# Linear attention with a rational feed-forward layer: the low words of 28 slots on GpSimd, Square and Ln in two buffers, another order

## The chip, the cores and the metric

The kernel runs on one core of one Trainium2 chip. The metric is the device time of one execution in microseconds (us). A core has five engines that run beside each other, each in its own program order: TensorE (PE in the profile), VectorE (DVE), ScalarE (ACT), GpSimd (POOL) and SyncE (SP), which here issues most DMAs.

## The reference, cut to what matters

A linear attention with decay over 4 x 8 heads of 768 steps gives x, 3072 tokens by 384. A feed-forward layer with a rational function of h follows.

```python
for t in range(S):
    cur = einsum('bhd,bhe->bhde', u * k[t], v[t])
    y[t] = einsum('bhd,bhde->bhe', r[t], state + cur)
    state = w * state + einsum('bhd,bhe->bhde', k[t], v[t])
...
h = x @ w_in                       # 3072 x 2048
P = a[0] + a[1]*h + a[2]*h*h + a[3]*h*h*h
Q = 1 + |b[0]|*|h| + |b[1]|*h*h
out = (P / (Q + 1e-6)) @ w_out     # 3072 x 384
```

## The kernel before

**Attention.** The 768 steps of each of 4 batches are cut into 6 blocks of 128, which makes 24 blocks n. For each block SP loads r, k and v (tasks Lr, Lk, Lv, and LV for a copy of v in another layout). r and k are scaled by powers of the decay (sr, sk), the bonus term is formed (ba, bb, bs, bv), PE transposes (tk, tr) and multiplies (a, kv, y), and ACT or DVE move results out of PSUM (tke, tre, ae, kve, ye). ca carries the state on. x turns the result, and xh and xl split it into a high and a low word, since each product of the feed-forward layer is made of three passes: high by high, high by low and low by high.

**Feed-forward.** Two blocks make a tile of 256 tokens, 12 tiles in all. The 2048 columns of h are worked on in 50 slots s (the table SL), most of them 1024 wide: four groups of 128 columns by 256 tokens. f1 (L644) makes h in PSUM, 9 matmuls of 256 columns for each group. Only two buffers of PSUM hold h (h0 and h1, in turn), so f1 of slot s+2 waits until the buffer of slot s is free. Then come ten instructions on the whole slot:

| task | line | engine | does | writes |
|---|---|---|---|---|
| z | L670 | ACT | absolute value of h | q |
| q | L674 | ACT | Square, so that q is Q without its last constant | q |
| t | L679 | ACT | Square of h, shifted | z |
| u3 | L691 | DVE | (t + constant) * h: P without its last constant | h, in PSUM |
| ln | L683 | ACT | Ln of q | z |
| ex | L687 | ACT | Exp(-z), which is 1/Q | z |
| hi | L696 | DVE | (h + constant) * z: the high word of P/Q | g |
| p | L700 | DVE | (q + constant) * g | q |
| d | L704 | DVE | h + constant - q: what the high word leaves over | h, in PSUM |
| lo | L709 | DVE | h * z: the low word | l |

t and ln share a buffer: ln overwrites what t wrote, so it waits until u3 has read it. q, z, g and l lie in seven SBUF buffers of 1024 columns (tags ta0 to ta6). f2 (L648, L649, L650) multiplies the two words by w_out, in two halves of 128 tokens, 12 matmuls of 384 columns each; the lines are high by high, high by low and low by high. os moves a finished half out of PSUM (L756 on ACT, L760 on DVE) and od stores it (L764).

**Weights.** w_in and w_out come as 64-bit numbers, in 28 pieces. Each is loaded by cl, turned into float32 by c0, cu (ACT), c2, c3 (DVE) and cr (POOL), and split by ch (ACT) and co (L420).

**Order.** Nothing is scheduled at build time. A string, ORDER, lists some 1840 tasks, each with the letter of its engine (D, A, G, P, S) and its buffer, and each engine takes its tasks in that order. The task warm.n (L797) is n matmuls on a constant, whose result nobody reads; they stand where PE has nothing else to do.

Of the kernel before, what the change touches and what calls it, by code (L numbers as in the profile page):

```python
# [49 lines left out]
pad.1G coefS plG mskG st0.0G st0.1G idG pad.0G wS Lv.3S betaA uwS ubG warm.54P ubpPpa0 cl_D ctrA st0.2A st0.3A Lv.2S LV.1.1.0A  # L50
LV.1.0.0A Lr.1S sqD Lr.2S pad.2G pow.0D pow.1D warm.10P turn.0.0Ppa1 warm.6P turn.1.0P inv.0D Lr.0S ubeA warm.13P turn.0.1Ppa0
pow.2D LV.1.0.1A Lk.0S Lk.2S warm.4P turn.2.0P tab.0A sr.1G inv.1D inv.2D warm.29P turn.2.1P Lk.1S Lv.0S LV.1.1.1A wlD turn.1.1P
tab.1A cl.2S tr.1Ph0 tre.1.0A tre.1.1A sr.0D wpPpa1 w128A cl.5S sr.2D sk.0D sk.2D ba.2Dm0 tr.0Ppa0 tre.0.1A warm.9P kv.2Ph1 sk.1D
tre.0.0A kve.2.0A bb.2D ba.0Dm1 Lr.3S ba.1Gm2 bs.2D bv.2D Lv.1S tk.0Ph0 tke.0A c0.2A c2.2Dh0 bb.1G kv.0Ppa1 kve.0.1A warm.2P
a.0Ppa0 bb.0G kve.2.1A warm.6P tk.1Ph1 c3.2D cu.2A cr.2Gta0 Lk.3S cl.6S tke.1A warm.16P a.1Ph0 kve.0.0A tk.2Ppa1 ae.0.1D cl.12S
bs.0D c0.5A ch.2A ae.0.0D bv.0G bs.1D LV.0.1.1A cl.1S ae.1.0D Lr.4S c2.5Dh1 LV.0.0.1A LV.0.0.0A ae.1.1D warm.36P kv.1Ph0 cl.4S
sr.3G c3.5D LV.0.1.0A y.0Ppa0 sk.3G ba.3Dm3 co.2D c0.6A bb.3D Lk.5S ca.0.1G cu.6A Lk.4S kve.1.0A c2.6Dh1 tke.2A ye.0D ca.0.0G
kve.1.1A c3.6D cr.6Gta1 c0.12A c2.12Dh0 c3.12D bv.1D warm.7P tr.2Ppa1 warm.2P kv.3Ppa0 c0.1A c2.1Dh1 c3.1D tre.2.0A cu.12A
cr.12Gta2 tre.2.1A bs.3D warm.13P x.0Ph0 cl.26S kve.3.0A kve.3.1A cu.5A warm.11P a.2Ppa1 ae.2.0D sr.4G y.1Ph1 tr.3Ppa0 ch.12A
cl.0S cu.1A sk.5G ae.2.1D ca.1.1G c0.4A warm.5P y.2Ppa1 ye.1D tk.3Ph1 xh.0A sk.4D tre.3.1A ca.1.0D xl.0D warm.3P tr.4Ph0 c0.26A  # L60
Lr.5S tre.3.0A tke.3A cr.5Gta3 ye.2D ba.4Dm1 c0.0A ch.6A warm.2P x.2Ppa0 xh.2A bv.3G c2.26Dh1 c3.26D cu.4A cr.1Gta4 xl.2D a.3Ppa1
warm.2P tk.4Ph1 ae.3.1D tre.4.0A sr.5G cl.20S Lv.5S tre.4.1A warm.21P kv.5Ph0 bb.4G cl.3S cl.9S ch.5A co.5G ae.3.0D c2.0Dpa0 c3.0D
ch.1A co.1G Lv.4S cu.20A tke.4A bs.4D c0.20A cl.10S cu.3A cl.11S kve.5.1D cu.0A cr.0Gta5 c2.4Dpa1 c3.4D cr.4Gta6 warm.16P x.1Ph1
xh.1A c0.3A xl.1D a.4Ppa0 warm.20P kv.4Ph1 cu.9A c2.3Dpa1 c3.3D cl.15S ch.0A co.0G cr.3Gta0 cu.26A cr.26Gta3 cl.14S cl.8S kve.5.0D
kve.4.1D c0.10A c2.10Dh0 c3.10D kve.4.0D warm.3P tk.5Ppa1 tke.5A cu.10A warm.14P y.3Ppa1 ye.3D c0.11A cu.11A ch.3A ba.5Gm0 c0.15A
f1.0.0Ph0 bv.4G LV.2.0.0S c2.11Dpa1 c3.11D cr.11Gta4 cu.15A LV.2.1.1S x.3Ph1 xh.3A ch.26A c0.9A c2.15Dpa1 c0.14A f1.0.1P f1.0.2P
bb.5G co.26G LV.2.1.0S ch.11A xl.3D tr.5Ph1 tre.5.1A tre.5.0A c3.15D co.12G ae.4.1D LV.2.0.1S ae.4.0D Lr.6S c2.14Dpa1 bs.5D
f1.0.3P warm.6P f1.1.0Ph1 cl.24S Lr.7S c3.14D z.0Ata5 c2.20Dpa0 c3.20D t.0Ata3 u3.0D warm.7P a.5Ppa1 ch.4A cu.8A cl.27S warm.1P
y.4Ppa0 cl.7S cl.13S ae.5.0D q.0A ln.0A f1.1.1P co.6G bv.5G cr.15Gta2 ch.15A ye.4D warm.5P x.4Ppa0 xh.4A cr.20Gta1 ch.20A Lk.6S
ae.5.1D warm.6P y.5Ppa1 sr.6D ex.0A cl.21S xl.4D warm.1P tr.6Ppa0 tre.6.0A tre.6.1A co.15G co.20G f1.1.2P f1.1.3P cl.18S ye.5D  # L70
c0.7A hi.0Dta2 x.5Ppa0 cl.17S sr.7G p.0D d.0D co.4G c0.8A z.1Ata1 xh.5A xl.5D tr.7Ppa1 tre.7.0A tre.7.1A co.3G lo.0Dta5 warm.54P
f1.2.0Ph0 f1.2.1P t.1Ata6 c2.9Dpa0 cr.10Gta0 ch.10A sk.6G cl.25S u3.1D co.10G co.11G Lr.8S c2.8Dpa1 f1.2.2P f1.2.3P ca.2.1G c3.9D
q.1A ln.1A ex.1A c0.17A c3.8D cr.8Gta3 cu.13A c2.7Dpa0 cl.16S cu.14A f2.0.0P f2.0.1P cl.22S cl.23S Lk.7S c0.13A hi.1Dta0 tk.6Ppa1
Lk.8S cu.7A ch.8A os.0.0A c3.7D z.2Ata4 t.2Ata2 ca.2.0G p.1D d.1D lo.1Dta5 co.8G cr.7Gta1 c2.17Dpa0 c3.17D sr.8G c2.13Dh1 os.0.1A
warm.23P f2.1.0P f2.1.1P q.2A cr.9Gta6 ch.7A co.7G Lv.8S u3.2D c0.16A c2.16Dpa0 c3.16D c3.13D ch.9A co.9G ca.3.0G warm.6P
f1.3.0Ph1 c0.18A c2.18Dpa0 c3.18D ln.2A ex.2A c0.23A cu.17A cr.14Gta3 cu.23A tke.6A c0.21A os.1.0A ch.14A Lv.6S warm.1P kv.6Ppa0
hi.2Dta0 p.2D d.2D lo.2Dta5 cu.16A cr.13Gta1 ch.13A co.13G co.14G c2.21Dpa1 kve.6.1D sk.7G f1.3.1P f1.3.2P f1.3.3P t.3Ata6 z.3Ata4
q.3A warm.16P f1.4.0Ph0 f1.4.1P c3.21D a.6Ppa1 u3.3D ln.3A ex.3A kve.6.0D ba.6Gm2 Lk.9S os.1.1A ba.7Gm3 Lr.10S c2.23Dpa0 ae.6.0D
cr.16Gta2 ch.16A c3.23D hi.3Dta1 p.3D f1.4.2P f1.4.3P t.4Ata3 c0.25A warm.1P tk.7Ppa0 f2.2.0P os.2.0A co.16G d.3D sk.8G bb.7G
Lv.7S c0.27A bb.6G lo.3Dta2 LV.3.0.1S f2.2.1P z.4Ata4 u3.4D q.4A ln.4A ex.4A ae.6.1D warm.8P f1.5.0Ph1 f1.5.1P f1.5.2P f1.5.3P  # L80
bs.6D os.2.1A f2.3.0P cr.23Gta6 ch.23A co.23G bs.7D c2.27Dpa1 c3.27D hi.4Dta0 c0.22A c2.22Dpa1 t.5Ata5 p.4D d.4D f2.3.1P cu.25A
# [855 lines left out]
```

## Time and profile before

| | |
|---|---|
| runs | 567.09 us (median of 3; 566.33 to 570.7) |
| the profiled execution | 566.86 us, its span 565.1 us |
| mean granted TensorE clock | 0.997 |
| busy | PE 550.0, DVE 471.7, ACT 397.0, POOL 163.1 us |
| loaded and stored | 29.01 MB and 4.72 MB |

The span runs from the first to the last instruction; 1.8 us of the execution lie outside it. Busy time of PE counts a matmul from its start to a modelled end, and since matmuls overlap, a short wait between two of them does not show in it. A wait is put down to the engine and line that released it.

### The profile page before, as it was taken

The page shows a single profiled execution, that of the slowest core. Times are in us where ns is not written, and L with a number is a line of the kernel's source. Part 1 is how long each engine was busy: PE and PEld are TensorE (multiplying, and loading weights), DVE is VectorE, ACT ScalarE, POOL GpSimd, SP SyncE. Part 2 cuts the span into 40 slices and gives each one's busy share as a digit, 9 for nine tenths or more (in the row PEclk, how much of TensorE's full clock was granted, in tenths as well). Part 3 has the DMA queues.
Part 4 walks back from the last instruction along what each step waited for, and adds up shares of the span by engine and source line. Part 5 has one row for each costly group of instructions (what it writes and reads, how often), then busy time and mean ns, then how long its engine had stood idle before and what let it go on. Part 6 is the DMA issues. An engine that isn't in the chain of part 4 may idle for free.

```text
span 565.1 us, 13792 instructions
## 1 busy us (share of the span) xinstructions
PE 550.0 (97%) x5916; PEld 527.3 (93%) x5916; DVE 471.7 (83%) x576; ACT 397.0 (70%) x522; POOL 163.1 (29%) x189
## 2 busy tenths in 40 slices
...
POOL 5689776688323143132121010001100100100000
PEclk9999999999999999999999999999999999999998
...
DMA packets 95273, 34.69 MB, mean 61 GB/s; under 512 B 88546, under 2 KB 91620, under 8 KB 95204
## 3 DMA queue, kind: packets, MB, share of 16 engines
...
q14 instruction: 21, 0.17, 0.1%
HBM read 29.01 MB, written 4.72 MB: 60 GB/s over the span
## 4 chain that ended last, share of the span: by engine, by line
PE 71%; DVE 17%; ACT 6%; issue 3%; POOL 1%; DVEq 0%; ACTq 0%; POOLq 0%
PE h L644 26%; PE o L648 8%; PE o L650 8%; PE o L649 8%; PE y L600 4%; DVE q L700 4%; PE a L550 4%; DVE g L696 4%; PE kv L572 4%; DVE h L704 3%; PE idle_bank L797 3%; DVE h L691 3%; ACT z L683 2%; ACT z L687 2%; PE tk L527 2%
## 5 line engine op out<-in xcount | busy, mean ns | idle before, releaser
L644 PE MATMUL h<-xthi,wi 128*128 128x256 f32 x1152 | 218.3, 284 | 2.4 <-DVE l L709 2.1
L644 PEld LDWEIGHTS h<-xthi,wi 128*128 128x128 f32 x1152 | 180.6, 188 | 6.7 <-PE o L650 2.2
L644 PE MATMUL h<-xtlo,wi 128*128 128x256 f32 x576 | 160.8, 279 | 0.0
L648 PE MATMUL o<-wo,g 128*128 128x384 f32 x384 | 132.4, 345 | 0.0
L650 PE MATMUL o<-wo,l 128*128 128x384 f32 x384 | 129.5, 337 | 1.0 <-DVE l L709 1.0
L649 PE MATMUL o<-wo,g 128*128 128x384 f32 x384 | 129.2, 336 | 0.0
L644 PEld LDWEIGHTS h<-xtlo,wi 128*128 128x128 f32 x576 | 108.4, 188 | 0.0
L696 DVE SCALAR_TENSOR_TENSOR g<-h,sig,z 128x1024 fp32r<-128x1024 f32 (+2 forms) x50 | 61.9, 1238 | 47.1 <-ACT z L687 46.4
L679 ACT ACTIVATE z<-h,off,root 128x1024 f32<-128x1024 f32 (+2 forms) x50 | 58.6, 1172 | 42.6 <-PE h L644 34.2
L683 ACT ACTIVATE z<-q,sig 128x1024 f32<-128x1024 f32 (+2 forms) x50 | 56.0, 1119 | 30.6 <-DVE h L691 29.5
L670 ACT ACTIVATE q<-h 128x1024 f32<-128x1024 f32 (+2 forms) x50 | 49.5, 990 | 38.8 <-PE h L644 27.0
L650 PEld LDWEIGHTS o<-wo,l 128*128 128x128 f32 x384 | 72.2, 188 | 1.5 <-DVE l L709 1.5
L648 PEld LDWEIGHTS o<-wo,g 128*128 128x128 f32 x384 | 72.2, 188 | 0.8 <-ACT os L756 0.2
L649 PEld LDWEIGHTS o<-wo,g 128*128 128x128 f32 x384 | 72.3, 188 | 0.0
L691 DVE SCALAR_TENSOR_TENSOR h<-z,sig,h 128x1024 f32<-128x1024 f32 (+2 forms) x50 | 62.0, 1240 | 5.5 <-ACT z L679 3.0
L700 DVE SCALAR_TENSOR_TENSOR q<-q,sig,g 128x1024 f32<-128x1024 f32 (+2 forms) x50 | 64.6, 1292 | 1.9
L704 DVE SCALAR_TENSOR_TENSOR h<-h,sig,q 128x1024 f32<-128x1024 f32 (+2 forms) x50 | 62.5, 1250 | 1.6
L709 DVE TENSOR_TENSOR l<-h,z 128x1024 fp32r<-128x1024 f32 (+2 forms) x50 | 59.1, 1181 | 2.8 <-DVE h L704 0.5
L674 ACT ACTIVATE q<-q,off,root 128x1024 f32<-128x1024 f32 (+2 forms) x50 | 60.6, 1211 | 1.1
L687 ACT ACTIVATE z<-z 128x1024 f32<-128x1024 f32 (+2 forms) x50 | 51.4, 1027 | 1.5
L522 POOL TENSOR_TENSOR m<-vn,dt 128x384 f32<-128x384 f32 x16 | 15.3, 962 | 121.9 <-DVE dt L518 121.9
L508 POOL TENSOR_TENSOR m<-rh,kh 128x384 f32<-128x384 f32 x17 | 17.4, 1028 | 101.0 <-DVE rh L504 48.1
...
## 6 DMA issues: line engine op xcount, KB each, us to landing
...
coef<-in_moe_a_dram SPq DMA_DIRECT2D x1, 2.0 KB, 2.6
```

Source lines behind the costliest of these rows:

```text
L644: nc.tensor.matmul(o, wi_of(j, cc, part), x_[:, cc], start=(n == 0), stop=(n == 3 * NCC - 1))
L648: nc.tensor.matmul(o, hi, wo_of(j, HI), start=first, stop=False)
L649: nc.tensor.matmul(o, hi, wo_of(j, LO), start=False, stop=False)
L650: nc.tensor.matmul(o, lo, wo_of(j, HI), start=False, stop=last)
L674: nc.scalar.activation(g["q"], g["q"], AF.Square, scale=RB, bias=KB)
L683: nc.scalar.activation(g["z"], g["q"], AF.Ln, bias=QE)
L687: nc.scalar.activation(g["z"], g["z"], AF.Exp, scale=-1.0)
L691: nc.vector.scalar_tensor_tensor(g["h"], g["t"], KAP, g["h"], op0=ALU.add, op1=ALU.mult)
L696: nc.vector.scalar_tensor_tensor(g["hi"], g["h"], c0, g["z"], op0=ALU.add, op1=ALU.mult)
L700: nc.vector.scalar_tensor_tensor(g["q"], g["q"], qe, g["hi"].bitcast(F32), op0=ALU.add, op1=ALU.mult)
L704: nc.vector.scalar_tensor_tensor(g["h"], g["h"], c0, g["q"], op0=ALU.add, op1=ALU.subtract)
L709: nc.vector.tensor_mul(g["lo"], g["h"], g["z"])
```

## The change

1. d writes its result to q, in SBUF, and not to h, in PSUM. So the buffer of h is free after d, where before it was free after lo. lo is now q * z, two operands in SBUF.
2. lo takes an engine from ORDER: 28 of the 50 are on POOL (G), 22 on DVE.
3. t writes to a buffer of its own, t. ln takes a new buffer z, so it no longer waits for u3. A slot then uses five buffers (q, t, z, g, l) of the same seven, t and z for a shorter time.
4. The last three slots (512, 256 and 256 columns) share buffers: slot 47 has one for q, t and z and one for g and l, slots 48 and 49 together the same. Slot 49's h lies in the second half of slot 48's PSUM buffer. Within them t and z have the same place, as before.
5. od takes an engine: the last but one store is issued by ACT.
6. ORDER is another one. PE has the same tasks but for the constant matmuls: 393 in 26 places, 439 in 37 before. Among the rest, the four clearings of the state (st0) are all on POOL (two were on ACT), co is on DVE 7 times (once before), LV is on ACT 19, DVE 9 and SP 20 times (22, 3 and 23 before).

```diff
-        g["z"] = g["t"] = ew_tile(s, "z")
+        g["t"] = ew_tile(s, "t")
         nc.scalar.activation(g["t"], g["h"], AF.Square, scale=RA, bias=KA)
...
+        g["z"] = ew_tile(s, "z")
         nc.scalar.activation(g["z"], g["q"], AF.Ln, bias=QE)
...
-        nc.vector.scalar_tensor_tensor(g["h"], g["h"], c0, g["q"], op0=ALU.add, op1=ALU.subtract)
+        nc.vector.scalar_tensor_tensor(g["q"], g["h"], c0, g["q"], op0=ALU.add, op1=ALU.subtract)
...
-    def ew_lo(s):
+    def ew_lo(s, e):
         g["lo"] = ew_tile(s, "l", F32R)
-        nc.vector.tensor_mul(g["lo"], g["h"], g["z"])
+        e.tensor_mul(g["lo"], g["q"], g["z"])
...
     def f1(s, jj):
-        if jj == 0:
+        if s == NS - 1:
+            hps[s] = hps[s - 1][:, GW // 2 : GW]
+        elif jj == 0:
             hps[s] = ps_h.tile([P, GW], F32, tag=here[0], name=f"h{s}")
...
+    packs = {}
+    PACK = {NS - 3: (0, 0), NS - 2: (1, 0), NS - 1: (1, 2 * N1)}
...
+        if s in PACK:
+            place, at_ = PACK[s]
+            key = place, dt
+            if key not in packs:
+                packs[key] = ew.tile([P, GW], dt, tag=here[0], name=f"{nm}{s}")
+            return packs[key][:, at_ + n * (nm in "tzl") : at_ + n * (nm in "tzl") + n]
...
-        nc.sync.dma_start(out[ds(bi * S + i * P, P), :], oss.pop((f, hf)))
+        e.dma_start(out[ds(bi * S + i * P, P), :], oss.pop((f, hf)))
...
-hi.43Dta2 p.43D d.43D lo.43Dta3 f1.44.0Ph0 f1.44.1P f1.44.2P f1.44.3P t.44Ata4
+ex.39A u3.39D hi.39Dta0 p.39D t.40Ata5 d.39D f2.38.0P f2.38.1P z.40Ata1 q.40A
+f1.41.0Ph1 f1.41.1P f1.41.2P f1.41.3P lo.39Gta5 f2.39.0P os.39.0A
```

In the rows below the name of a buffer ends in its slot and a running number: q39_6162 is q of slot 39. The first place is late in the program, DVE's work on slots 39 and 40, before:

```order
L691 SCALAR_TENSOR_TENSOR h39_6091<-z39_6136,sig_102,h39_6091 128x1024
L696 SCALAR_TENSOR_TENSOR g39_6156<-h39_6091,sig_102,z39_6136 128x1024
L700 SCALAR_TENSOR_TENSOR q39_6138<-q39_6138,sig_102,g39_6156 128x1024
L704 SCALAR_TENSOR_TENSOR h39_6091<-h39_6091,sig_102,q39_6138 128x1024
L709 TENSOR_TENSOR l39_6160<-h39_6091,z39_6136 128x1024
L508 TENSOR_TENSOR m22_6172<-rh1_109,kh1_110 128x384
L561 TENSOR_TENSOR ysb0_115<-a22_6228,mask_82 64x512
L691 SCALAR_TENSOR_TENSOR h40_6162<-z40_6261,sig_102,h40_6162 128x1024
```

Five instructions a slot, the last of them lo. The same place after the change:

```order
L704 SCALAR_TENSOR_TENSOR h39_6034<-t39_6188,sig_102,h39_6034 128x1024
L709 SCALAR_TENSOR_TENSOR g39_6236<-h39_6034,sig_102,z39_6165 128x1024
L713 SCALAR_TENSOR_TENSOR q39_6162<-q39_6162,sig_102,g39_6236 128x1024
L717 SCALAR_TENSOR_TENSOR q39_6162<-h39_6034,sig_102,q39_6162 128x1024
L704 SCALAR_TENSOR_TENSOR h40_6167<-t40_6239,sig_102,h40_6167 128x1024
L709 SCALAR_TENSOR_TENSOR g40_6290<-h40_6167,sig_102,z40_6286 128x1024
L713 SCALAR_TENSOR_TENSOR q40_6266<-q40_6266,sig_102,g40_6290 128x1024
L562 TENSOR_TENSOR ysa1_116<-a23_6269,mask_82 64x512
```

Four a slot: u3 (now L704), hi (L709), p (L713) and d (L717). p of slot 40 stands two instructions behind d of slot 39. POOL has the low words (L722) between what is left of the attention's work for the last blocks, after the change:

```order
L722 TENSOR_TENSOR l34_5737<-q34_5646,z34_5649 128x1024
L514 TENSOR_TENSOR m22_5759<-m22_5759,ub_86 128x384
L523 TENSOR_TENSOR m21_5307<-vn21_4421,dt21_5868 128x384
L722 TENSOR_TENSOR l36_5990<-q36_5832,z36_5835 128x1024
L722 TENSOR_TENSOR l37_6012<-q37_5943,z37_5970 128x1024
L523 TENSOR_TENSOR m22_5759<-vn22_5190,dt22_6150 128x384
L722 TENSOR_TENSOR l39_6346<-q39_6162,z39_6165 128x1024
```

Before, POOL had only the small rows (m) there. The third place is again DVE after the change, at slot 34, whose low word is on POOL:

```order
L717 SCALAR_TENSOR_TENSOR q34_5646<-h34_5542,sig_102,q34_5646 128x1024
L562 TENSOR_TENSOR ysb0_115<-a20_5509,mask_82 64x512
L514 TENSOR_TENSOR m23_5705<-m23_5705,ub_86 128x384
L562 TENSOR_TENSOR ysa1_116<-a21_5741,mask_82 64x512
L509 TENSOR_TENSOR m22_5759<-rh1_109,kh1_110 128x384
```

One instruction behind d of slot 34 stands a bonus product (bb, L514), with two operands in SBUF.

More of the change, by code (lines that the diff above doesn't have):

```diff
@@ L49 @@
 ORDER = """
[L50 to L81, printed above, removed]
@@ L163 @@
-d.47D lo.47Dta4 z.48Ata5 f2.46.0P q.48A t.48Ata6 u3.48D ln.48A f2.46.1P ex.48A hi.48Dta3 p.48D f1.49.0Ph1 z.49Ata0 t.49Ata1 q.49A
-u3.49D ln.49A ex.49A d.48D lo.48Dta5 hi.49Dta6 p.49D d.49D lo.49Dta0 flagtPpa1 flagmD f2.47.0P f2.47.1P f2.48.0P f2.48.1P f2.49.0P
-f2.49.1P os.49.0A od.11.0S os.49.1A od.11.1S
+wS plG coefS Lr.0S mskG idG Lv.3S pad.0G uwS pad.1G Lr.1S Lv.2S st0.1G cl_D ctrA pow.0D inv.0D warm.42P turn.0.1Ppa0 st0.2G pow.1D
+inv.1D warm.9P turn.1.1P turn.0.0Ppa1 betaA ubG st0.3G pad.2G pow.2D inv.2D turn.2.0P wlD Lk.2S Lr.2S Lk.0S turn.1.0P tab.0A
@@ new lines @@
+warm.14P ubpPpa1 sr.0D sr.1D LV.1.0.1A LV.1.1.0A turn.2.1P tab.1A sk.2D warm.24P tr.0Ppa0 tr.1Ph0 kv.2Ph1 cl.5S LV.1.1.1A st0.0G
+sr.2D sk.0G ubeA tre.0.1A tre.1.0A ba.2Dm0 bb.2D bs.2D Lk.1S tre.0.0A LV.1.0.0A wpPpa1 cl.2S bv.2G kve.2.1A kve.2.0A warm.9P
+tk.0Ppa0 tke.0A Lv.0S c0.5A cu.5A cl.6S sqD warm.25P a.0Ph1 Lv.1S tre.1.1A c0.2A warm.16P kv.0Ph0 cl.1S ba.0Gm1 Lr.3S ae.0.0D
+bb.0G sk.1G tk.1Ppa0 ae.0.1D ba.1Gm2 w128A c2.2Dpa1 c3.2D cu.2A c0.6A kve.0.1A kve.0.0A bb.1G cr.2Gta0 c2.6Dh1 tke.1A c2.5Dh0
@@ new lines @@
+c3.5D LV.0.0.0A warm.16P kv.1Ppa1 cr.5Gta1 bs.1D bv.1G c3.6D Lk.3S a.1Ppa0 tk.2Ph0 ae.1.0D sr.3G LV.0.0.1A LV.0.1.1A cl.12S Lk.4S
+Lk.5S LV.0.1.0A ch.5A tke.2A kve.1.0A bs.0D bv.0D sk.3G cu.6A cr.6Gta2 cl.4S warm.15P y.0Ph1 tr.2Ph0 ca.0.0G ye.0D tre.2.1A co.5D
+ae.1.1D tre.2.0A warm.10P x.0Ph1 xh.0A c0.1A ba.3Dm3 bb.3G Lr.5S sk.4G warm.11P a.2Ph0 kve.1.1A xl.0D c0.12A c2.1Dpa0 ae.2.0D
+warm.5P kv.3Ppa1 cu.1A sk.5G ae.2.1D cu.12A c3.1D cr.1Gta3 Lr.4S y.1Ph1 tr.3Ph0 ca.1.0G ye.1D tk.3Ppa0 cl.3S kve.3.0A c0.4A
@@ new lines @@
+c2.4Dh1 kve.3.1A sr.5G cl.26S cl.0S y.2Ppa1 tre.3.0A tke.3A c3.4D sr.4G tre.3.1A ye.2D ch.2A cu.4A ca.1.1G cu.3A c2.12Dh1 co.2D
+c3.12D Lv.5S warm.11P a.3Ppa0 ae.3.1D ae.3.0D c0.3A cu.26A x.2Ph0 cl.11S xh.2A xl.2D Lv.4S warm.8P x.1Ph1 xh.1A xl.1D c0.26A
+cr.12Gta4 ch.1A tr.4Ppa1 ba.5Gm1 co.1G c0.0A bb.5G c2.26Dpa0 warm.19P tk.4Ph0 tke.4A kv.5Ph1 cl.15S tre.4.1A c3.26D cr.26Gta5
+cl.20S c2.3Dpa0 c2.0Dh0 tre.4.0A warm.21P a.4Ppa1 kve.5.0D cl.9S c3.0D kve.5.1D c3.3D cu.0A ch.6A cl.8S ca.0.1G warm.10P kv.4Ph0
@@ new lines @@
+cr.0Gta6 c0.11A c2.11Dh1 ch.26A ch.12A cu.11A c0.15A cl.10S ch.0A tk.5Ppa0 tke.5A c3.11D ba.4Gm0 kve.4.0D warm.12P y.3Ph1 c0.20A
+cu.20A bs.3D cu.15A tr.5Ppa0 kve.4.1D ae.4.0D c0.9A bv.3D co.0G LV.2.0.1S ae.4.1D tre.5.1A c2.15Dpa1 cr.11Gta1 ch.11A cu.9A bs.5D
+c3.15D bb.4G tre.5.0A LV.2.0.0S LV.2.1.1S cu.10A cr.4Gta0 LV.2.1.0S warm.2P f1.0.0Ph0 f1.0.1P f1.0.2P f1.0.3P c0.10A c0.8A ye.3D
+warm.3P x.3Ppa1 cl.7S ch.4A co.11G co.6G c2.10Dpa0 Lr.6S cr.3Gta3 z.0Ata6 cl.14S a.5Ph1 bs.4D xh.3A bv.4G q.0A cl.13S Lr.7S c3.10D
@@ new lines @@
+cr.15Gta1 co.26D ae.5.0D t.0Ata2 ae.5.1D warm.1P y.4Ppa0 ln.0Ata5 xl.3D warm.26P f1.1.0Ph1 f1.1.1P c2.20Dpa1 u3.0D cl.27S bv.5G
+co.4G ch.3A cl.16S ex.0A ye.4D y.5Ppa0 sr.6G cu.8A cl.23S c3.20D cr.20Gta2 c0.14A c0.7A hi.0Dta0 ye.5D co.12G Lr.8S tr.6Ppa1
+tre.6.0A warm.12P x.4Ppa0 Lk.6S tre.6.1A sr.7G cr.10Gta4 xh.4A f1.1.2P ch.20A p.0D cl.25S ch.15A co.15G x.5Ppa1 xh.5A d.0D c0.13A
+xl.4D ch.10A Lv.6S warm.16P tr.7Ph0 co.3D tre.7.0A f1.1.3P tre.7.1A xl.5D warm.9P f1.2.0Ph0 f1.2.1P f1.2.2P z.1Ata1 q.1A c2.9Dpa0
@@ new lines @@
+c3.9D t.1Ata3 c2.8Dpa1 c3.8D cl.24S Lv.9S c2.14Dpa0 co.20G lo.0Gta2 f2.0.0P sk.6G cr.8Gta6 c2.7Dpa1 Lk.7S ba.6Gm2 Lr.9S u3.1D
+ln.1Ata5 ex.1A f1.2.3P ca.2.0G cu.14A hi.1Dta3 p.1D d.1D co.10G cu.7A c0.16A ch.8A f2.0.1P os.0.0A t.2Ata4 co.8G bb.6G z.2Ata0
+os.0.1A q.2A lo.1Dta2 cl.18S c3.7D c2.13Dh1 cr.9Gta6 warm.47P f2.1.0P f2.1.1P cl.19S u3.2D c2.16Dpa1 cl.17S cr.7Gta1 ch.9A co.9G
+cu.13A c3.14D ch.7A co.7G ln.2Ata5 ex.2A c3.13D c3.16D Lv.7S tk.6Ppa0 hi.2Dta3 p.2D d.2D tke.6A cr.14Gta2 c0.23A c2.23Dpa1 c3.23D
```

180 lines of the change are left out of this document (95 added, 85 removed).

## The prediction

> **What bounds the kernel.** I read the page first: busy times and the slices of the span.
>
> ```profile
> span 565.1 us, 13792 instructions
> PE 550.0 (97%) x5916; PEld 527.3 (93%) x5916; DVE 471.7 (83%) x576; ACT 397.0 (70%) x522; POOL 163.1 (29%) x189
> POOL 5689776688323143132121010001100100100000
> PEclk9999999999999999999999999999999999999998
> ```
>
> PE is busy for 97% of the span and its clock is whole throughout. POOL does little in the second half, which is where most of the new low words go. The busy time by stretch of the program says where the other engines could hold PE up (columns: length, then PE, weight loads, DVE, ACT and POOL):
>
> ```profile
> 0.00:60.00 60.00, 56.73 (x1044) 51.92 (x1046) 52.57 (x107) 53.12 (x110) 42.48 (x61) 1.00 0.97 236
> 110.00:200.00 90.00, 90.00 (x1078) 85.95 (x1076) 84.59 (x105) 62.52 (x81) 45.21 (x52) 1.00 0.29 54
> 300.00:400.00 100.00, 99.91 (x837) 98.02 (x836) 79.38 (x78) 67.88 (x69) 6.71 (x7) 1.00 0.09 21
> ```
>
> In the first 60 us PE, DVE and ACT are all full. From 110 to 200 us DVE has 84.6 of 90 us, from 300 to 400 us it has 20 us to spare; PE is full in both. So a shorter load on DVE or ACT is worth nothing by itself: only what PE does without need, or waits for, can be won. What it does without need are the constant matmuls of warm, in their groups by form and in one piece of the chain that ended last:
>
> ```profile
> L797 PE MATMUL idle_bank<-wones 128*128 128x128 bf16 x384 | 27.9, 226 | 2.4 <-POOL wones L242 2.4
> L797 PE MATMUL o<-wones 128*128 128x128 bf16 x55 | 4.1, 220 | 1.2 <-ACT os L756 1.2
> 22.02 2.01 PE idle_bank L797 x36
> ```
>
> 384 and 55 make the 439 of ORDER. 36 of them take 2.01 us, 56 ns each, so all take 24.6 us. They end at about 100 us: behind that PE has real work to the end. What PE waits for, from the view of waits (total, times, longest):
>
> ```profile
> PE h L644 <- DVE l L709: 2.1, 4, 1.0
> PE x L619 <- DVE m L605: 1.2, 1, 1.2
> PE o L797 <- ACT os L756: 1.2, 1, 1.2
> PE o L650 <- DVE l L709: 1.0, 1, 1.0
> ACT z L683 <- DVE h L691: 29.5, 34, 2.7
> ```
>
> That is 5.5 us of PE. The last row is ACT's: 34 times ln waits for u3. The split of t and z takes that wait away, but PE doesn't see it except where the whole chain of a slot is late.
>
> **The change, part by part.** I sum against the profiled execution: span 565.1, 1.8 us more as executed, 566.9 us; the median of the runs is 0.2 above it.
>
> *Constant matmuls.* 46 fewer by 56 ns: 2.6 us less. This holds only if what they waited for comes earlier. In the first 60 us one thing does: ACT loses two clearings of the state.
>
> ```profile
> L456 ACT COPY vs<-zero 64x576 f32<-64x576 f32 x4 | 2.7, 666 | 0.1
> ```
>
> The 2.7 us lie ahead of everything that ACT does for the first block, and go to POOL, whose first tasks were short. Against it stand six more co on DVE, which is as full. I take the 2.6 us, with nothing as one end and, were all of ACT's 2.7 us to come on top, 5.3 us as the other.
>
> *PE's waits for lo.* h is now free after d, so f1 two slots on can start one lo earlier; before, it waited up to 1.0 us for it. And the end of the program:
>
> ```profile
> 538.77 1.22 DVE L709 TENSOR_TENSOR l<-h,z 128x1024 fp32r<-128x1024 f32 x1
> 540.13 0.36 PE L644 MATMUL h<-xthi,wi 128*128 128x256 f32 x1 [0.98 <-DVE l L709]
> 557.65 0.42 DVE L709 TENSOR_TENSOR l<-h,z 128x256 fp32r<-128x256 f32 x1
> 553.12 0.28 PE L644 MATMUL h<-xthi,wi 128*128 128x256 f32 x1
> 556.29 0.34 PE L649 MATMUL o<-wo,g 128*128 128x384 f32 x1
> 556.47 0.34 PE L650 MATMUL o<-wo,l 128*128 128x384 f32 x1
> 558.13 0.45 PE L650 MATMUL o<-wo,l 128*128 128x384 f32 x1 [0.96 <-DVE l L709]
> 559.22 1.66 SPq L764 DMA_DIRECT2D out_dram<-os x2
> ```
>
> At 540.1 f1 of slot 47 waits for lo of slot 45; at 558.1 the last f2 waits for the last lo, since f1 of slot 49 stood behind f2 of slot 46. Now slot 49's f1 follows slot 48's, ahead of f2 of 46, 47 and 48 (24, 12 and 6 matmuls 0.175 us apart by the rows at 556.3 and 556.5: 7.4 us). That covers its chain, which took 5.0 us from the last matmul of f1 (553.12) to the end of lo (557.65 + 0.42). Both rows go: 2.1 + 1.0 = 3.1 us. What is late next is d itself, 1.2 us earlier; the new order uses some of that up by calling f1 earlier, so I don't count it twice. The two last stores are issued one behind the other in 1.66 us; on two queues, and with the second os on DVE, I count 0.3.
>
> *The waits of x and warm.* These two, 1.2 us each, belong to places that no longer exist. An order of this length makes others: I take half, 1.2 us, with 0 and 2.4 as ends.
>
> *lo on POOL.* No row has POOL at 1024 columns. The nearest:
>
> ```profile
> L420 POOL TENSOR_TENSOR wo<-bwo,wo 128x384 fp32r<-128x384 f32 x16 | 17.8, 1124 | 7.1 <-ACT wo L417 7.0
> L420 POOL TENSOR_TENSOR wi<-bwi,wi 128x512 fp32r<-128x512 f32 x11 | 14.5, 1321 | 10.5 <-ACT wi L417 10.4
> L709 DVE TENSOR_TENSOR l<-h,z 128x1024 fp32r<-128x1024 f32 x47 | 57.5, 1224 | 2.3
> L696 DVE SCALAR_TENSOR_TENSOR g<-h,sig,z 128x1024 fp32r<-128x1024 f32 x47 | 60.2, 1281 | 44.3 <-ACT z L687 43.6 <-PE o L649 0.4
> L700 DVE SCALAR_TENSOR_TENSOR q<-q,sig,g 128x1024 f32<-128x1024 f32 x47 | 62.9, 1338 | 1.7
> ```
>
> 128 columns more cost 0.20 us, so 1024 cost 1.32 + 4 x 0.20 = 2.1 us; in proportion to 512 they cost 2.64. I take 2.4. DVE is freed of 28 x 1.22 = 34 us, POOL takes 67 us, which it has; a low word on POOL comes 1.2 us later than on DVE. In the new order f2 stands 12.6 us of PE's work or more behind f1, mostly over 14, wherever lo of a whole slot is on POOL, so that costs nothing by itself.
>
> *Two operands in SBUF.* Here is a cost that the busy times don't show. p (L700) reads q and g, both in SBUF; the other four DVE instructions of a slot read h in PSUM. These rows are from DVE's and POOL's order of time, two places:
>
> ```profile
> 96.62 1.92 DVE L700 SCALAR_TENSOR_TENSOR q<-q,sig,g 128x1024 f32<-128x1024 f32 x1
> 97.41 2.02 POOL L500 TENSOR_TENSOR kh<-kh,wkn 128x384 f32<-128x384 f32 x1
> ...
> 211.95 1.49 DVE L611 TENSOR_TENSOR vs<-vs,w 48x192 f32<-48x192 f32 x2
> 213.47 1.27 DVE L500 TENSOR_TENSOR kh<-kh,wkn 128x384 f32<-128x384 f32 x1
> ...
> L500 POOL TENSOR_TENSOR kh<-kh,wkn 128x384 f32<-128x384 f32 x14 | 15.3, 1093 | 7.1 <-PE h L644 3.9 <-DMA kh<-in_k_dram 3.2
> L500 DVE TENSOR_TENSOR kh<-kh,wkn 128x384 f32<-128x384 f32 x10 | 6.1, 622 | 0.8 <-DMA kh<-in_k_dram 0.8
> ```
>
> A POOL instruction that comes during p takes 2.02 us where its mean is 1.09, and ends 0.9 us behind p: it did its work after it. p itself took 1.92 there, not 1.28, having met a POOL instruction at its start; at 213.5 DVE's scaling of k took twice its mean while POOL was at work. So the two engines take turns where DVE has two operands in SBUF. The change lets POOL hold that place 2.4 us at a time, and makes each lo that stays on DVE (22) such an instruction too. In the new order p stands two instructions (2 x 1.28 = 2.56 us) behind d where slots follow closely, as at slots 39 and 40: POOL's 2.4 us just fit. At twelve slots a smaller instruction with two operands in SBUF stands nearer, as at slot 34. Taking 2.4 us less the DVE work in between, they could hold DVE up by 16 us in all. How much reaches PE? Before, the 1.0 us lost by DVE at 212 to 215 us and some 2.7 us on p (47 x (1338 - 1281) ns) stand against one wait of PE, 1.2 us, for what DVE did next (x for m): a third at most, 5.4 us of 16. DVE is 34 us lighter now, so I take 2.5, with 0 and 5.4 as ends.
>
> The Trainium skill's GPSIMD Engine Reference, section 8 (Key points), names this: GpSimd shares its SBUF interfaces with VectorE and contends with instructions that have two SBUF inputs. The trace agrees, with 1.92 for 1.28 us. By the page's other advice (section 4.1, Engine selection: elementwise work on VectorE, GpSimd about twice as slow with two inputs) the move is wrong, and the sum would be the slow rival's below; by the trace POOL is 2.4 / 1.22, twice as slow too, but off the path.
>
> **The sum:** 565.1 - 2.6 - 3.1 - 0.3 - 1.2 + 2.5 = 560.4; as executed 562.2, by the median 562.4 us, 0.8% less. With the ends of the terms it runs from about 557 to 568. A difference under 1% is about what a measurement of this kernel can't tell from none.
>
> **The rivals.**
> 1. *Everything is won:* POOL and DVE never meet, the waits of x and warm go without successors, ACT's 2.7 us come on top. 565.1 - 2.6 - 2.7 - 3.1 - 0.3 - 2.4 = 554.0, by the median 556.0 us. For it speaks that ACT is full in the first 60 us; against it, that DVE and the loads are as full.
> 2. *The constant matmuls were only cover,* and the change doesn't do what it says: what PE waited for comes no earlier, the 2.6 us turn into waits, and d is as late as lo was because the order calls f1 earlier. Only 0.3 to 1 us is left: 566.5 us. For it speaks that a constant matmul stands where PE would wait anyway; against it, the two rows of the end.
> 3. *Slower: POOL's low words hold DVE up, and DVE holds up PE.* The places are the twelve above, and slots 24 and 39, where p of the next slot is due 2.56 us after d. There a low word decides that takes over 2.56 us with its start (2.64 is the upper price), or that still has an attention product ahead of it on POOL: then p and d wait, and f1 of the second next slot waits for d with little to spare. If all 16 us reach PE: 562.4 - 2.5 + 16.2 = 576 us; it is slower by 1% (572.8) from 12.9 us on, four fifths. Against it: DVE's spare time, and that the order leaves p its place.
>
> **Chances.** The forecast's case 0.54, spread over 558.5 to 568 and even on both sides of a gain of 1% (561.4 us); rival 1 0.17, rival 2 0.16, rival 3 0.13. Faster by over 1%: 0.27 + 0.17 = 0.44; within 1%: 0.27 + 0.16 = 0.43; slower: 0.13. The range 555.5 to 570 leaves out rival 3 and little else.
>
> **What would show it.** Right: PE's constant matmuls at 22 us, no wait of f1 for DVE over 0.5 us near the end, the last f2 without a wait; lo on POOL at 2.2 to 2.6 us, longer only where it starts during p; some p of 1.5 us and more in slots 3 to 21. Wrong: waits of PE for POOL's l, p with a mean over 1.6 us (rival 3), new waits of PE in the first 100 us (rival 2), or a granted clock under 0.99.

## The result, and the profile after

The changed kernel takes 573.40 us (median of four runs, 572.27 to 576.66) against 566.97 us before: ratio 1.0114, 95% interval 1.0076 to 1.0151. It is slower by about 1.1%. 562.4 was predicted, with 570 as the upper end.

The page after begins so; the profiled execution took 573.43 us:

```profile
span 571.7 us, 13762 instructions
PE 549.7 (96%) x5870; PEld 529.0 (93%) x5870; DVE 469.9 (82%) x566; ACT 388.1 (68%) x511; POOL 231.9 (41%) x216
PEclk9799999999997999999999999999999999999998
```

The clock row is new: in two slices of 14.3 us, the second and the thirteenth, it falls to 0.7. DVE, which was to be 34 us lighter, is lighter by 1.8. What PE waits for (total, times, longest):

```profile
PE x L620 <- DVE m L606: 3.7, 1, 3.7
PE kv L573 <- ACT vs L424: 3.5, 1, 3.5
PE o L810 <- ACT os L769: 1.9, 1, 1.9
PE h L645 <- DVE q L717: 1.1, 2, 0.9
```

The last two rows answer to rows of before: f1's wait for DVE has fallen from 2.1 to 1.1 us, and the last f2's has no row any more. The first two are new in their size. They lie in the two slices where the clock fell. By stretches (length, PE busy, granted clock; the last two columns are DMA), about either wait:

```profile
20.00:23.00 3.00, 0.21 (x4) 0.94 1.14 237
23.00:26.00 3.00, 2.26 (x44) 0.50 0.08 27
26.00:29.00 3.00, 3.00 (x38) 0.50 0.34 66
...
171.00:174.00 3.00, 0.95 (x32) 0.80 0.34 66
174.00:177.00 3.00, 1.30 (x13) 0.50 0.00 0
177.00:180.00 3.00, 3.00 (x34) 0.56 0.02 5
```

Behind each wait PE works at about half clock for four to six microseconds, so a wait costs more than its length. The Trainium skill, "TensorE: Matmul & The Clock Gate", Part 1, states such a rule with a figure: no PE-idle gaps over about 3.4 us. These two, 3.5 and 3.7 us, are over it and agree.

**Place 1, near 24 us.** kv.1 can begin when c3.2 on DVE (L409) is done, since that frees the PSUM buffer it writes to; the view names ACT, whose copies ended at 23.1 us. DVE's order of time, and below it POOL's:

```profile
15.52 0.93 DVE L277 TENSOR_TENSOR root<-root,half 128x2 f32<-128x2 f32 x1
18.59 0.99 DVE L285 SCALAR_TENSOR_TENSOR off<-ctmp,half 128x2 f32<-128x2 f32 x1
19.61 0.16 DVE L286 TENSOR_TENSOR half<-off 128x2 f32<-128x2 f32 x1
22.95 0.69 DVE L409 SCALAR_TENSOR_TENSOR swi<-swi,c 128x512 int32<-128x512 int32 x1
...
15.43 1.00 POOL L509 TENSOR_TENSOR m<-rh,kh 128x384 f32<-128x384 f32 x1
18.55 1.01 POOL L509 TENSOR_TENSOR m<-rh,kh 128x384 f32<-128x384 f32 x1
```

These are the squares of the prologue (sq), on two numbers a row. A clean one takes 0.16 us (L286); the two above it take 0.93 and 0.99, and each begins just behind the start of a POOL product of 1.0 us and ends just behind its end. In all the fifteen small instructions of sq take 6.4 us here, 14.5 to 20.9. In the old order it stood 10 us earlier, where POOL had fills and one product, and they took 2.9. No low word is involved: the order moved sq into the bonus products.

**Place 2, near 172 us.** Here one is. DVE's and POOL's order of time, and PE's next step:

```profile
160.44 2.09 DVE L505 TENSOR_TENSOR rh<-rh,wrn 128x384 f32<-128x384 f32 x1
165.68 2.01 DVE L713 SCALAR_TENSOR_TENSOR q<-q,sig,g 128x1024 f32<-128x1024 f32 x1
169.38 0.41 DVE L424 COPY vs<-vn 64x192 f32<-64x192 f32 x2
170.29 3.23 DVE L424 COPY vs<-vn 64x192 f32<-64x192 f32 x2
173.55 1.34 DVE L523 TENSOR_TENSOR m<-vn,dt 128x384 f32<-128x384 f32 x1
174.99 0.56 DVE L606 TENSOR_TENSOR m<-y,m 128x384 f32<-128x384 f32 x1
...
170.09 2.35 POOL L722 TENSOR_TENSOR l<-q,z 128x1024 fp32r<-128x1024 f32 x1 [2.03 <-DVE vs L424]
172.39 1.01 POOL L509 TENSOR_TENSOR m<-rh,kh 128x384 f32<-128x384 f32 x1
...
175.70 0.87 PE L620 MATMUL x<-identw,m 128*128 128x128 f32 x3 [3.74 <-DVE m L606]
```

The scaling of r at 160.4, which takes 0.56 us where it is clean, had met the low word of slot 8. Two copies of V slices take 0.41 us at 169.4. The next two start 0.2 us into the low word of slot 9 and take 3.23: the first goes when the low word ends, the second when the attention product behind it ends. bv (L523) meets one more attention product. ye (L606), for which x.8 waits, ends at 175.6. In the groups, the copies after and before, the low words and p:

```profile
L424 DVE COPY vs<-vn 64x192 f32<-64x192 f32 x18 | 14.4, 841 | 0.2
L722 POOL TENSOR_TENSOR l<-q,z 128x1024 fp32r<-128x1024 f32 x26 | 63.2, 2433 | 146.8 <-PE o L650 43.5 <-DVE q L717 42.2 <-ACT q L682 25.6
L713 DVE SCALAR_TENSOR_TENSOR q<-q,sig,g 128x1024 f32<-128x1024 f32 x47 | 63.3, 1347 | 1.6
```
```profile
L423 DVE COPY vs<-vn 64x192 f32<-64x192 f32 x6 | 3.2, 573 | 0.0
```

There are three times as many copies on DVE as before, and each takes longer. p, on which the prediction had its eye, takes 1347 ns on average, as before (1338).

### The profile page after: what moved, and what is told of

It is laid out like the page before. It is cut to its first block, busy times and chain, and to the rows that moved or that the text cites. A ratio compares the mean times of both kernels' runs of the same rounds, so it can differ in the third digit from the quotient of the medians.

```text
span 571.7 us, 13762 instructions
## 1 busy us (share of the span) xinstructions
PE 549.7 (96%) x5870; PEld 529.0 (93%) x5870; DVE 469.9 (82%) x566; ACT 388.1 (68%) x511; POOL 231.9 (41%) x216
## 4 chain that ended last, share of the span: by engine, by line
PE 70%; DVE 13%; ACT 7%; issue 3%; POOL 3%; DMA 2%; SPq 2%; DVEq 0%; POOLq 0%; ACTq 0%
PE h L645 26%; PE o L649 10%; PE o L651 9%; PE o L650 9%; PE a L551 4%; PE y L601 3%; PE kv L573 3%; DVE q L713 2%; DVE g L709 2%; DVE vs L424 2%; PE tk L528 1%; PE tr L528 1%; PE idle_bank L810 1%; ACT z L696 1%; DMA swi<-in_moe_w_in_dram 1%
## 5 line engine op out<-in xcount | busy, mean ns | idle before, releaser
L651 PE MATMUL o<-wo,l 128*128 128x384 f32 x376 | 126.7, 337 | 0.0
L722 POOL TENSOR_TENSOR l<-q,z 128x1024 fp32r<-128x1024 f32 x26 | 63.2, 2433 | 146.8 <-PE o L650 43.5
L704 DVE SCALAR_TENSOR_TENSOR h<-t,sig,h 128x1024 f32<-128x1024 f32 x47 | 60.3, 1283 | 23.0 <-ACT t L691 19.2
L709 DVE SCALAR_TENSOR_TENSOR g<-h,sig,z 128x1024 fp32r<-128x1024 f32 x47 | 60.2, 1281 | 21.4 <-ACT z L700 15.8
L691 ACT ACTIVATE t<-h,off,root 128x1024 f32<-128x1024 f32 x47 | 56.5, 1202 | 25.1 <-PE h L645 18.0
L713 DVE SCALAR_TENSOR_TENSOR q<-q,sig,g 128x1024 f32<-128x1024 f32 (+2 forms) x50 | 65.0, 1301 | 1.7
L717 DVE SCALAR_TENSOR_TENSOR q<-h,sig,q 128x1024 f32<-128x1024 f32 (+2 forms) x50 | 62.0, 1240 | 1.5
L696 ACT ACTIVATE z<-q,sig 128x1024 f32<-128x1024 f32 x47 | 54.0, 1150 | 9.7 <-PE o L650 3.9
L700 ACT ACTIVATE z<-z 128x1024 f32<-128x1024 f32 x47 | 49.8, 1060 | 1.1
L523 POOL TENSOR_TENSOR m<-vn,dt 128x384 f32<-128x384 f32 x17 | 15.5, 912 | 71.3 <-DVE dt L519 63.1
L551 PEld LDWEIGHTS a<-ysa,kt 64*64 64x64 f32 x384 | 25.7, 142 | 6.9 <-issue 3.8
```

The lines of the kernel that those rows point to most:

```text
L651: nc.tensor.matmul(o, lo, wo_of(j, HI), start=False, stop=last)
L691: nc.scalar.activation(g["t"], g["h"], AF.Square, scale=RA, bias=KA)
L696: nc.scalar.activation(g["z"], g["q"], AF.Ln, bias=QE)
L704: nc.vector.scalar_tensor_tensor(g["h"], g["t"], KAP, g["h"], op0=ALU.add, op1=ALU.mult)
L709: nc.vector.scalar_tensor_tensor(g["hi"], g["h"], c0, g["z"], op0=ALU.add, op1=ALU.mult)
L713: nc.vector.scalar_tensor_tensor(g["q"], g["q"], qe, g["hi"].bitcast(F32), op0=ALU.add, op1=ALU.mult)
```

## The experiments

Two theories stand. **A:** some instructions of DVE can't begin while POOL's product runs, and this, at two places, with the clock that falls behind each, is the whole loss. **B:** DVE and the loads are simply too full in the new order. All kernels are the changed one with the edit shown (tasks of ORDER; D, A and G are DVE, ACT and POOL).

**Each place by itself.** First the squares put 10 us later, behind bv.0, then two V-slice copies of pair 5 (two instructions each) given to ACT, and then both:

```diff
-cl.6S sqD warm.25P
+cl.6S warm.25P
...
-bv.0D sk.3G
+bv.0D sqD sk.3G
...
-LV.5.0.1D
+LV.5.0.1A
...
-LV.5.1.0D
+LV.5.1.0A
```

The first two hunks are e1_sq, the other two e2_lv, all four e3_both.

> The changed kernel, with only the 15 tiny DVE instructions of pro_squares (sq) moved in the order, from ahead of ae.0 to between bv.0 and ye.0, where DVE idles 1.7 us. Theory A (DVE is held up by POOL; each tiny product with two operands in SBUF waits up to 0.8 us for POOL's running instruction, 6.4 us for the 15, so c3.2 frees its buffer late and PE waits 3.5 us ahead of kv.1, after which its clock is halved for some 6 us): the wait ahead of kv.1 falls under 1 us, the clock stays whole up to 60 us, and the time falls by 4 to 6.5 us, to 567 to 569.5 us. Theory B (the wait ahead of kv.1 comes from the loads: the chain that ended last leads through a piece of w_in, 6.7 us to land): the wait stays over 3 us and the time within 1 us of 573.4.

> The changed kernel, with only two copies of v (LV.5.0.1 and LV.5.1.0, two instructions each) taken from DVE to ACT at the same place of the order, at 169 to 174 us, where ACT idles 3.4 us. Theory A (DVE's fast copies are held up by POOL's low word: 3.23 us for two that take 0.4 us at 169.4; PE then waits 3.7 us for m ahead of x.8, and its clock is halved for some 6 us): the wait ahead of x.8 falls to about 1 us, the clock stays whole there, and the time falls by 4 to 5 us, to 568.5 to 569.5 us. Theory B (DVE is simply too full there, whoever makes the copies; the low word or the scaled r of the next blocks come as late): the wait falls by no more than the copies' own 0.8 us, and the time by 1 us at most.

> The changed kernel with both moves, sq and the two copies of v. Theory A: the two gains add up, 8 to 11.5 us, to 562 to 565.5 us, which is the sum of the prediction (562.4 us) and below the kernel before; granted clock 0.997 as before. Theory B: 571.5 to 574 us.

Measured: e1_sq 572.8 us (ratio to before 1.0090, 1.0064 to 1.0116), e2_lv 567.23 (0.9989, 0.9966 to 1.0012), e3_both 566.77 (0.9982, 0.9957 to 1.0007). In their views of waits, in that order of kernels (lines are nine lower, the table being shorter):

```profile
PE x L611 <- DVE m L597: 6.3, 2, 3.7
```
```profile
PE kv L564 <- issue: 2.3, 1, 2.3
```
```profile
PE x L611 <- DVE m L597: 2.9, 1, 2.9
```

The copies bear the theory out: without those four instructions the wait of 3.7 us is gone, and 6.2 us with it. Not all of that need be theirs. In the execution of e2_lv that was profiled PE came to kv.1 a microsecond later, so the wait there is 2.3 us where it was 3.5, though kv.1 itself begins at 23.6 as before; the half clock behind it lasts 3.4 us and not 6.8, which is worth up to 1.7 us. The squares missed: the wait for kv.1 went, but a new one of 2.6 us in e1_sq and of 2.9 in e3_both stood ahead of x.0, since sq met POOL's products at its new place as well (0.75 and 0.78 us for 0.16) and ye.0 stood behind it. So e3_both stayed above the range that A gave.

**The squares where POOL has no products.** sq right behind the scaling of r for block 1, alone (e9_sq) and with the two copies on ACT (e6_sq_lv); and with all nine LV of DVE given to ACT (e10_all).

```diff
-sr.0D sr.1D LV.1.0.1A
+sr.0D sr.1D sqD LV.1.0.1A
...
-cl.6S sqD warm.25P
+cl.6S warm.25P
```

> The changed kernel with the squares of the prologue alone moved behind the second row preparation; the V-slice copies stay on VectorE. If the two places act apart, this gives what the run with both moves won over the run with the copies alone, 5.8 us: 567 to 568.5, with the wait ahead of kv.1 gone and the wait of 3.7 us ahead of x.8 still there. If they act together (a late start pushes the copies under the low word), it gives more or less than that: 562 to 565 with the second wait gone, or 571 to 573.

> The changed kernel with two moves: the squares of the prologue (sq) stand on VectorE right behind the second row preparation (sr.1), where GpSimd has only memory fills in its queue, and the two V-slice copies of block 5 go from VectorE to ScalarE. Theory A (two places where GpSimd holds VectorE up make the whole loss, with the clock halved behind each): the waits of about 3.5 us ahead of kv.1 and 3.7 us ahead of x.8 both go, no new one of over 2 us stands ahead of x.0, the clock is 0.99 or more; time 562 to 565, 8 to 11 us under the changed kernel and 2 to 5 under the one before. Theory B (the squares are late because of what they wait for, not because of GpSimd): the products of sq stay at 0.6 to 1.0 us each wherever they stand, and the time stays at the 567 of the run with the copies alone.

> As the run with the squares behind sr.1, and all nine V-slice copies that stand on VectorE go to ScalarE. Theory A: no V-slice copy on VectorE is left to be held up, so beside the waits ahead of kv.1 and x.8 the small ones near 158 and 287 us go too, 1 to 2 us more; time 561 to 564. Rival: ScalarE, busy 68% and in its own tight order there, takes seven more copies of about 0.4 us and hands its exponentials or other results over later; the time is equal to the run with two copies moved, or 1 to 3 us more.

Measured: e9_sq 567.32 us (0.9991, 0.9965 to 1.0016; kv.1 runs at 20.7 there, before ACT's V-slice copies, 21.1 to 23.6, have begun, so it doesn't need these), e6_sq_lv 561.45 (0.9899, 0.9855 to 0.9943), e10_all 562.12 (0.9888, 0.9845 to 0.9932). The page of e6_sq_lv, its longest wait for DVE, and DVE's time at the squares with POOL's fill beside it:

```profile
span 559.8 us, 13762 instructions
PEclk9999999999999999999999999999999999999999
```
```profile
PE h L645 <- DVE q L717: 1.1, 2, 0.9
```
```profile
9.51 0.16 DVE L277 TENSOR_TENSOR root<-root,half 128x2 f32<-128x2 f32 x1
...
9.41 1.20 POOL L459 MEMSET vs<- 64x576 f32 x2
```

The product that took 0.93 us takes 0.16 beside POOL's fills. The two places act apart: -6.1 us for the squares, -6.2 for the copies, -12.0 for both; e9_sq and e6_sq_lv, which differ by the copies alone, are 5.9 us apart. So the two placements alone make the change slower; with both mended the rest of it is 5 us faster than before (566.48 in the same comparison). The seven other copies win nothing: no wait that counts stood behind them.

**The clock's share.** Fifty constant matmuls ahead of kv.1 and of x.8, which keep PE busy while it waits:

```diff
-warm.16P kv.1Ppa1
+warm.16P warm.50P kv.1Ppa1
...
-ye.8D x.8Ppa1
+ye.8D warm.50P x.8Ppa1
```

> The changed kernel with 50 constant matmuls (2.8 us at full clock) put ahead of kv.1 and 50 ahead of x.8, so that PE computes during most of the two long waits; everything else is as in the changed kernel, and what PE waits for comes no earlier. If the halved clock behind the waits is what costs part of the time (theory A's second half): the granted clock returns to 0.99 or more and the time falls by 2.5 to 5 us, to 568.5 to 571 us. If the clock does not matter, because PE waits there for others anyway: within 1 us of 573.4 us, or above it by what the filler holds up.

Measured: 570.57 us (1.0051, 1.0030 to 1.0073). In the profiled execution, which took 568.75, the clock is whole at both places; over the ten it is 0.995 to 0.999. In e4_warm's stretches, to be held against the 0.50 above:

```profile
26.00:29.00 3.00, 3.00 (x58) 1.00 0.81 169
```

So by the medians 2.8 of the 12 us go with the clock (4.7 in the profiled execution); the rest is the waits and what they push back.

**Is it POOL, or is DVE too full?** All 28 low words back on DVE (e5_lodve), and the low word of slot 9 alone (e7_lo9):

```diff
-lo.9Gta4
+lo.9Dta4
```

> The changed kernel, its order of tasks kept, with all 28 low words put back on VectorE (the same multiplication, q by z from SBUF). VectorE gets some 26 multiplications of about 1.26 us, 33 us more work, and GpSimd 63 us less. Theory A (GpSimd's low words hold VectorE's instructions up, most of all copies and two-operand products from SBUF): the copies of V slices fall from a mean of 0.84 us to about 0.3, the product p from 1.35 to about 1.2; the wait ahead of x.8 near 172 us falls from 3.7 us to under 1.5 us and the granted clock there comes back; time 564 to 571, not above the changed kernel's 573.4. The wait ahead of kv.1 near 24 us, where GpSimd has other work than low words, stays. Theory B (VectorE has too much to do in this order, whoever makes the low words): 33 us more on VectorE make the waits longer, time 577 or more.

> The changed kernel with one instruction moved: the low word of slot 9 is made by VectorE instead of GpSimd, at the same place of the order. Theory A (that one GpSimd multiplication holds the two V-slice copies near 170 us): VectorE does 1.26 us more there, and yet the copies take 0.25 us instead of up to 3.2, the wait ahead of x.8 falls from 3.7 to under 2.5 us and the half clock behind it goes; time 567 to 571, at least 2 us under the changed kernel. Theory B (VectorE is too full there): the wait ahead of x.8 grows to about 5 us and the time is 574 to 577.

Measured: e5_lodve 588.54 us (1.0367, 1.0325 to 1.0410), e7_lo9 574.83 (1.0121, 1.0075 to 1.0166). Both times are B's, and by much in the first, and the granted clock stays low (0.978 and 0.982 in the profiled executions). Yet the rows of the copies and of x.8's wait, which is gone or 0.2 us, are A's. p isn't: A had it falling to about 1.2 us, and in e5_lodve it took 1380 ns. The copies in e5_lodve, and what PE waited for there:

```profile
L424 DVE COPY vs<-vn 64x192 f32<-64x192 f32 x18 | 5.2, 328 | 0.2
```
```profile
PE o L651 <- DVE l L722: 5.1, 2, 3.8
```

In e7_lo9 the copies come in the same order, and the low word only 8 us behind them, which the order's place for it allows:

```profile
169.21 0.43 DVE L424 COPY vs<-vn 64x192 f32<-64x192 f32 x2
...
176.94 1.23 DVE L722 TENSOR_TENSOR l<-q,z 128x1024 fp32r<-128x1024 f32 x1
178.22 0.69 PE L651 MATMUL o<-wo,l 128*128 128x384 f32 x1 [3.47 <-DVE l L722]
```

One multiplication taken from POOL turns 3.23 us of copies into 0.43, and x.8's wait into 0.2. But DVE is behind with the low word itself then, and f2 of slot 9 waits 3.5 us in place of x.8. DVE's busy time shows the same from the other side: in e5_lodve its low words take 34 us more than in the changed kernel (60.9 for 26.5), and its busy time rises by 12.9 us only (482.8 for 469.9). So by these rows over 20 us of DVE's busy time in the changed kernel were hold-ups that went with POOL's low words. Both theories hold a part: POOL's product holds the copies up, and DVE is so full there that it can't take the product back. In this order the move to POOL is worth 15 us by itself (588.5 against 573.4). The Trainium skill's GPSIMD Engine Reference, section 4.1 (Engine selection), would have such work on VectorE; this run disagrees.

**How long a hold-up is.** A small kernel (m1_pair; nothing of the layer is computed) repeats eight kinds of DVE instructions.

> Not the layer: a small kernel that gives VectorE the same eight instructions again and again (copy 64x192, product 128x2 of two SBUF operands, scaling 128x2 of one, product 128x384, sum 128x384, three-operand instruction 128x1024 with both tensors in SBUF, the same with one in PSUM, product 128x1024), first alone, then while GpSimd multiplies 128x1024 from SBUF without a break, then while it multiplies 128x384, then while it fills memory. Theory A (a VectorE instruction of some kinds can't start until GpSimd's running product has ended): alone they take what the big kernel's clean ones take, 0.25, 0.15, 0.15, 0.5, 0.5, 1.3, 1.3 and 1.25 us; beside the 128x1024 products those held take up to 2.4 us more, beside the 128x384 ones up to 1.0 us more, beside the fills nothing more; held are the copy and the products of two SBUF operands, not the one with PSUM. Theory B (both engines share the port word by word): each VectorE instruction of those kinds grows by the same factor, 1.5 to 2, whatever GpSimd's instruction length, so the copy takes 0.4 to 0.5 us and never 2.

Its groups, first alone (8 to 46 us), then beside POOL's 128x1024 products (60 to 140), then beside its 128x384 ones (165 to 270):

```profile
L53 DVE SCALAR_TENSOR_TENSOR o_d<-h,s,y 128x1024 f32<-128x1024 f32 x8 | 10.2, 1271 | 0.0
L47 DVE COPY o_cp<-vn 64x192 f32<-64x192 f32 x8 | 2.0, 246 | 0.0
...
L69 POOL TENSOR_TENSOR l<-q,z 128x1024 fp32r<-128x1024 f32 x26 | 80.1, 3082 | 2.0
L52 DVE SCALAR_TENSOR_TENSOR o_p<-y,s,y 128x1024 f32<-128x1024 f32 x8 | 23.2, 2895 | 0.0
L54 DVE TENSOR_TENSOR o_big<-y,y 128x1024 fp32r<-128x1024 f32 x9 | 19.5, 2167 | 0.0
L47 DVE COPY o_cp<-vn 64x192 f32<-64x192 f32 x9 | 19.3, 2147 | 0.0
L53 DVE SCALAR_TENSOR_TENSOR o_d<-h,s,y 128x1024 f32<-128x1024 f32 x8 | 10.2, 1272 | 0.0
...
L71 POOL TENSOR_TENSOR g<-g,g 128x384 f32<-128x384 f32 x68 | 101.9, 1498 | 5.3
L47 DVE COPY o_cp<-vn 64x192 f32<-64x192 f32 x15 | 14.8, 986 | 0.0
```

The copy goes from 0.25 to 2.15 us beside long products and to 0.99 beside short ones: the hold-up follows the length of POOL's instruction, not that of the copy, as A says. The three-operand instruction with both tensors in SBUF takes 2.9, where p's clean rows have 1.28; the same with one in PSUM stays at 1.27. POOL pays too: 3.08 us where its low words in the changed kernel take 2.43, and 1.50 for its 128x384 products where they take 0.99 once DVE is done. Two things stay open. By A all products of two operands in SBUF should have been held. The one of 128x1024 was (2.17 us beside the long products, for 1.21 alone); those of 128x2 and 128x384 were not (0.14 and 0.54), nor was the sum (0.54). These always came right behind a copy that had just been let in, unlike the squares at place 1; whether that is the reason was not tried. And DVE was done before POOL's fills began, so that part measured nothing; the rows of e6_sq_lv stand for it.

**Shorter instructions on POOL.** Each of its low words in two multiplications of 128x512, in the changed kernel (e11_halves) and in e6_sq_lv (e12_best_halves):

```diff
-        e.tensor_mul(g["lo"], g["q"], g["z"])
+        n = g["lo"].shape[-1] // (2 if e is nc.gpsimd else 1); [e.tensor_mul(g["lo"][:, i : i + n], g["q"][:, i : i + n], g["z"][:, i : i + n]) for i in range(0, g["lo"].shape[-1], n)]
```

> The changed kernel, its order kept, with each low word that GpSimd makes cut into two multiplications of 128x512, one behind the other. Theory A (a VectorE instruction waits for the end of GpSimd's running instruction and then goes first): each hold-up by a low word falls from up to 2.4 us to up to 1.3; the two copies ahead of x.8 take 1.5 to 2.2 us instead of 3.2, the wait of 3.7 us falls below 3 us and the halved clock behind it goes; time 566 to 571. Theory B (VectorE waits until GpSimd's queue of products is empty, or is slowed word by word): the two copies take 3 us as before and the time stays at 573, or rises by the price of 26 more instructions on GpSimd where it is waited for.

> The run with both moves (561.45 us) with GpSimd's low words in halves as well. Theory A: the waits of TensorE that are left there are 0.9 us and less and only partly from low words; shorter hold-ups win 0 to 1.5 us: 560 to 561.5. Rival: 26 more instructions on GpSimd make its low words later by some 0.2 us each, and where the last ones are waited for the time grows: 562 to 564.

Measured: e11_halves 564.37 us (0.9928, 0.9901 to 0.9955), e12_best_halves 559.65 (0.9834, 0.9788 to 0.9879). Groups of e11_halves:

```profile
L722 POOL TENSOR_TENSOR l<-q,z 128x512 fp32r<-128x512 f32 x52 | 69.6, 1358 | 143.9 <-PE o L650 43.4 <-DVE q L717 35.8 <-ACT q L682 25.3
L424 DVE COPY vs<-vn 64x192 f32<-64x192 f32 x18 | 7.9, 478 | 0.2
```

POOL works 6.4 us more, the copies take 478 ns on average for 841, and the kernel is 9 us faster with no task moved; it is below the range that A gave. The copies ahead of x.8 now came before the low word and missed it altogether (0.43 us for the two). That they did is luck of this order, so the 9 us are not the price of length alone; in e12_best_halves, where those copies are on ACT, the cut is worth 1.8 us by the medians. e12_best_halves, with the two moves as well, is the fastest of all and 1.7% under the kernel before.

## Why the prediction was wrong, step by step

- **Constant matmuls (-2.6).** Right in count: 346 and 47, 393 for 439, 22 us by its 56 ns. But kv.1 waits 3.5 us in the same stage, which had no term. With that mended (e6_sq_lv) no wait over 0.4 us stands in the first 100 us but those of constant matmuls for wones at the start and for os.
- **PE's waits for lo (-3.1).** Right in kind: the last f2 waits no more, no f1 waits near the end. What is left is 0.9 us at 159.6 us, for d, plus 0.2, so 2.0 of the 3.1 us came.
- **Waits of x and warm (half of 2.4 won).** Wrong: x's grew from 1.2 to 3.7 us, warm's from 1.2 to 1.9.
- **lo on POOL.** Right: 2433 ns for the 2.4 taken, and PE never waits for it.
- **Two operands in SBUF (+2.5, ends 0 and 5.4).** This is the step that failed, in which instructions it counted and in its ends. It looked at p and at twelve products behind d. p kept its mean, and in slots 39 and 40 it took 1.28 us. The instructions whose hold-up reached PE were mostly of kinds it had not counted: the plain copy, which reads one operand, and the squares, too small to stand among the groups by cost. The count of copies on DVE was in the text of the change (LV 9 times on DVE, 3 before), and their mean of 573 ns before, over twice the 246 of a clean one, showed them held already; neither was read. The upper end, "a third at most" of DVE's hold-up, was taken from one place of before; at the two places most of it reached PE: at the first all 3.5 us of sq's, at the second 3.7 of 5.8 (scaling of r 1.5, p 0.7, copies 2.8, bv 0.8). With the clock behind them the two places cost 12.0 us (573.40 for 561.45 with both mended), where the term had 2.5.
- **The clock.** No term had it. The prediction named a granted clock under 0.99 as a sign against it, and 0.985 came; but a wait had been priced at its length. e4_warm puts 2.8 us on it.
- **DVE 34 us lighter.** It was lighter by 1.8: the hold-ups (over 20 us by e5_lodve), twelve more copies and the other moved tasks took back what the low words freed.
- **The range.** The ends of the terms, added up, give 556.0 to 569.1 us, not 557 to 568; 573.4 lies outside both.

Where these two places are mended the time comes close to the sum: 561.45 us measured, 562.4 predicted, span 559.8 for 560.4. This is in part luck. The sum holds 2.5 us for hold-ups, which the mending takes away, and without them it would be 559.9; against that, f1 still waits 1.1 us there, and of the waits of x and warm 0.5 us is won where 1.2 was counted. Of the rivals the slower one came true in kind (POOL holds DVE up, DVE holds PE up; 576 us), though not at slots 24 and 39 and not by p. Nor was it its price, all 16 us of those hold-ups: what came was two waits of other origin and the clock behind them. Which parts of the change make the 5 us by which it is faster with both places mended was told apart only for the move to POOL.
